# Gathering the expert rows in 512-byte halves and turning them on VectorE in a spectral mixture-of-experts kernel

## The chip, the cores and the metric

One Trainium2 chip, one core. The metric is the device time of one execution in microseconds. Below, TensorE is also called PE, VectorE DVE, ScalarE ACT, GpSimd POOL and SyncE SP, as the profile's rows do.

## What is computed

Two stages follow each other, all in float32:

```python
X = rfft(x, axis=1)                       # x: 8 x 1856 x 256
Yr = Xr @ w_r - Xi @ w_i + b_r            # and Yi, then a soft threshold of 0.01
y = irfft(Yr + 1j * Yi, n=1856, axis=1)   # 14848 rows of 256
g = argmax(y @ w_group); e = argmax(y @ w_expert[g])
h = relu(y @ w1[g, e])                    # 256 -> 1024
out = weight(g, e) * (h @ w2[g, e])       # 1024 -> 256, 16 experts, one per row
```

Each of the 14848 rows goes to one of 16 experts; its output row is the expert's, scaled by two softmax values.

## The kernel before

The first part (to about 440 us of the profile) does the transforms, the routing and the sorting. It writes the transformed rows to a DRAM tensor `ys_d` (one row of 256 values, 1024 bytes, per position) and, for each expert, a list of row numbers and weights to `lst`; the first 512 rows of experts 0 to 3 are worked on there too, in an order written out by hand.

The main part, from about 441 to 1050 us, is the one that the change touches. It works through 40 jobs, numbered 0 to 39 here: expert 3 (256 and 304 rows), expert 1 (432), expert 2 (400), then the largest of the other twelve experts ("rank 0": 384, 384, 336), expert 0 (256, 256), and ranks 1 to 11 with the sizes of `CUTS` (lines 38 to 40). A job's rows lie in tiles of up to 128. For job i the program of the loop at line 1410 says, in this order:

1. `fetch` (lines 535 to 549) gathers the rows of job i+1: for each tile one indirect DMA on GpSimd's queue, one row of 1024 bytes per partition, into tiles `xg` (three buffers of two tiles).
2. The first two tiles of job i-1 go through the second layer (`down_g`, lines 632 to 659: 16 matmuls per tile, then a scaling on ScalarE (L656) and one on VectorE (L657), then an indirect store, L625). The PSUM pool for this has two banks. Jobs of 288, 304, 320, 400 and 416 rows may be "turned": their second layer runs with weights stationary (`turned_g`, L673, one half in front of the first layer of the next job, one behind it) and its result is transposed back (`back_g`, L686) during a later job.
3. The first layer of job i (`up_g`, L578): eight groups of six matmuls; ScalarE takes the high part of the hidden values (L583), VectorE the low part (L585). In some jobs (`split_at`, two jobs ahead of an expert's first) the weights of a later expert are split in eight pieces between these, a cast on ScalarE (L524) and a subtraction on VectorE (L525); where the job has fewer than 384 rows, four of the eight come in the next job.
4. In the jobs that split weights, `dma_next` starts the loads of the expert after, and its row list (`rank_ids`, line 1324, with five small GpSimd operations in `indices`, lines 352 to 359).
5. The leftover tile of job i-1, if it has three, or the second half of a turned job.
6. `prep` (lines 551 to 567) turns the rows of job i+1, so that the 256 features lie on partitions: two TensorE transposes per tile (L561) into PSUM bank `pg`, then ScalarE copies the high part `xth` (L565) and VectorE subtracts to get the low part `xtl` (L566).

TensorE, ScalarE, VectorE and SyncE follow this program order. GpSimd's order is chosen by the compiler within the dependencies. `xq`, which holds `xth` and `xtl`, has two buffers of each. The output tiles `yo` have four. After the loop a flexible loop (line 1463) takes what did not fit in the jobs; it uses `fetch` and `prep` as well.

The core of `up_g`, whose operand order matters here (`w1h`, `w1l` are the high and low weights, stationary):

```python
for ch in range(2):
    for a_, b_ in ((w1h, xth), (w1h, xtl), (w1l, xth)):
        nc.tensor.matmul(o[:, :n], lhsT=a_[:, ch, fs], rhs=b_[:, ch, 0:n], ...)
```

Of the kernel before, what the change touches and what calls it, by code (L numbers as in the profile page):

```python
# [9 lines left out]
F32 = mybir.dt.float32  # L10
F32R = mybir.dt.float32r
# [122 lines left out]


@with_exitstack
def spectral_moe(ctx: ExitStack, tc: tile.TileContext, x, wri, bri, wgate, w1, w2, cst, out):
    nc = tc.nc

    dram = ctx.enter_context(tc.tile_pool(name="dram", bufs=1, space=bass.MemoryType.DRAM))  # L140
# [211 lines left out]
    def indices(ids, pool, both=True):  # L352
        if both:
            nc.gpsimd.tensor_copy(out=ids.gi, in_=ids.ent[:, :, 0])
        tmp = pool.tile([128, 12], F32, name="ixt", bufs=1)[:, 0:ids.n]
        nc.gpsimd.tensor_scalar(out=tmp, in0=ids.ent[:, :, 0], scalar1=0.0, scalar2=float(NPAD + 1), op0=ALU.is_equal, op1=ALU.mult)
        nc.gpsimd.tensor_scalar_add(out=tmp, in0=tmp, scalar1=-1.0)
        nc.gpsimd.tensor_tensor(out=tmp, in0=tmp, in1=ids.ent[:, :, 0], op=ALU.add)
        nc.gpsimd.tensor_copy(out=ids.si, in_=tmp)

    class Ids:
        def __init__(self, ent, gi, si):
            self.ent, self.gi, self.si, self.n, self.last = ent, gi, si, gi.shape[1], 128

        def cut(self, a_, b_):
            part = Ids(self.ent[:, a_:b_], self.gi[:, a_:b_], self.si[:, a_:b_])
            if b_ == self.n:
                part.last = self.last
            return part
# [134 lines left out]
        nc.sync.dma_start(out=lst[NE * CAP:ROWS], in_=zero[:, 0, :])  # L504
        nc.sync.dma_start(out=ys_d[0:1, :], in_=zero[0:1].rearrange("p c k -> p (c k)"))

    def raw_w(e):
        rows = slice(e * 128, e * 128 + 128) if isinstance(e, int) else bass.ds(e * 128, 128)
        raws = []
        for src in (w1, w2):  # L510
            raw = xp.tile([128, 2048], F32, name="xt")
            nc.sync.dma_start(out=raw, in_=src[rows])
            raws.append(raw)
        return raws
# [20 lines left out]
    def fetch(mp, ids, bufs, rows=NPAD + 1, late=False):  # L535
        n = ids.n
        out_ = []
        for c0 in range(0, n, 2):
            w = min(2, n - c0)
            xg = mp.tile([128, 2, D], F32, name="xg", bufs=bufs)  # L540
            for c in range(w):
                m = ids.rows(c0 + c)
                ins = nc.gpsimd.indirect_dma_start(  # L543
                    out=xg[0:m, c, :], out_offset=None, in_=ys_d[0:rows, :],
                    in_offset=bass.IndirectOffsetOnAxis(ap=ids.gi[0:m, c0 + c:c0 + c + 1], axis=0))
                if late:
                    behind(ins, "stores of the early jobs go first")
            out_.append((xg, w, ids.rows(c0 + w - 1)))
        return out_

    def prep(mp, xgs, n, bufs=None):
        xth = mp.tile([128, 2, n], F32R, name="xth", bufs=bufs)
# [768 lines left out]
    def ranked(k):  # L1321
        return nc.values_load(order_r[:, k:k + 1], engines=sp, min_val=0, max_val=NE - 1)

    def rank_ids(k, ek):
        rows = CUTS[k]
        n = sum((m + 127) // 128 for m in rows)
        ids = Ids(ft.tile([128, n, 2], F32, name=f"ent_r{k}"), ft.tile([128, n], I32, name=f"gi_r{k}"),
                  ft.tile([128, n], I32, name=f"si_r{k}"))
        if any(m % 128 for m in rows):
            nc.gpsimd.memset(ids.ent, 0.0)  # L1330
        parts = part_lists(ids, lambda r, n: bass.ds(ek * CAP + r, n), rows)
        indices(ids, ft)
        return parts

    def half_prep(xgs):
        (xg, _, _), = xgs
# [48 lines left out]
    def dma_next():  # L1385
        if not loads:
            return
        j = loads.pop(0)
        kind, q = jobs[j]
        if kind == "l":  # L1390
            raws[j] = raw_w(q[0])
        else:
            k = q[0]
            ek = ranked(k)
            raws[j] = raw_w(ek)
            rids[k] = rank_ids(k, ek)

    table = flex_table()
# [4 lines left out]
    def turned(i):  # L1403
        return 0 < i < len(jobs) - 1 and jids[i].rows() in TURNED and not turned(i - 1)

    prev, behind_, todo = None, iter(()), []
    x2 = prep(xq, first[0], jids[0].rows())
    for e in (3, 1, 2, 0):
        indices(fids[e][0], ft, False)
    for i, (kind, q) in enumerate(jobs):  # L1410
        ids = jids[i]
        if kind == "r":
            wt = wts["r", q[0]] = jw[i] if i in jw else wts["r", q[0]]
        else:
            wt = wts[q[0]] = jw[i] if i in jw else wts[q[0]]
        if i + 1 < len(jobs) and jobs[i + 1][0] == "r":
            k, part = jobs[i + 1][1]
            jids[i + 1] = rids[k][part]
        nxt = fetch(xp2, jids[i + 1], 3, late=i == 0) if i + 1 < len(jobs) else None
        rest, back = iter(()), behind_  # L1420
        behind_ = iter(())
        if prev is not None:
# [22 lines left out]
            emit(todo, len(todo))  # L1445
        if i == 0 or i in split_at:
            dma_next()
        drain(rest)
        prev = (hs, ids, wt)
        if nxt is not None:  # L1450
# [29 lines left out]
def _layout(x, w_r, w_i, b_r, b_i, w_group, w_expert, w1, w2):  # L1480
# [9 lines left out]
        wg[:, i, :, i, G:G + NE] = w_expert.reshape(G, 8, 32, EG).transpose(1, 2, 0, 3).reshape(8, 32, NE)  # L1490
    wg = np.tile(wg.reshape(8, 64, 64).transpose(1, 0, 2), (2, 1, 1))
    w1s = w1.reshape(NE, 2, 128, F).transpose(0, 2, 1, 3).reshape(NE * 128, 2 * F)
    w2s = w2.reshape(NE, 8, 128, D).transpose(0, 2, 1, 3).reshape(NE * 128, 8 * D)
    named = (("x", xs), ("wri", wri), ("bri", bri), ("wgate", wg.reshape(128, 512)), ("w1", w1s), ("w2", w2s))
    return [(n, np.ascontiguousarray(a)) for n, a in named]


# [19 lines left out]
```

## Time and profile before

| | |
|---|---|
| median of 3 runs | 1058.54 us (1057.88 to 1060.74) |
| the profiled execution | 1058.72 us, span 1056.9 us |
| TensorE | busy 1029.3 us (97%), clock 0.998 of full |
| VectorE | 674.9 us (64%) |
| ScalarE | 491.4 us (46%) |
| GpSimd | 427.3 us (40%) |

The span runs from the first to the last instruction of the core. A busy time is the sum over the times in which an instruction of that engine runs; matmuls are pipelined, so that one lasts longer than the step from its start to the next one's. [...] The chain of waits is followed back from the last instruction, at each step to what released it or to the instruction before it on its engine; what is not on it can change without moving the end until it gets there.

### The profile page before, as it was taken

Reading aid. Unit: us, or ns where it says so; the run is one execution under the profiler, and the core shown is the slowest. Engines: PE = TensorE matmul, PEld = TensorE weight load, DVE = VectorE, ACT = ScalarE, POOL = GpSimd, SP = SyncE. Lnnn points to the kernel's source line nnn. Section 1 sums busy time; section 2 is a strip of 40 time slices with the busy share of each in tenths; the row PEclk is TensorE's granted clock in tenths of the full one; section 3 lists DMA queues with packets and bytes.
Section 4 is the critical chain, followed back from the end, with each engine's and each line's share of the span. In section 5 each row is a group of like instructions: output and inputs, shape, how many; then the busy total and the mean of one; then the engine's idle time right before and its main releaser. Section 6 shows DMA issues by size and latency. Waiting matters only on the chain.

```text
span 1056.9 us, 24666 instructions
## 1 busy us (share of the span) xinstructions
PE 1029.3 (97%) x9688; PEld 901.7 (85%) x9688; DVE 674.9 (64%) x1610; ACT 491.4 (46%) x1273; POOL 427.3 (40%) x600
## 2 busy tenths in 40 slices
PE   8999999999999998999999999999999999999997
PEld 4886777776867887899999999999999999999996
DVE  6778999999898675455365555454645546545632
ACT  2564554554635343344354445444544435445532
POOL 0120162555374668553343433343433443342422
PEclk9999999999999999999999999999999999999999
DMA  9401512421414430233132231331313313233110
GB/s 383 153 3 52 210 62 82 156 88 59 146 60 152 142 110 22 64 133 101 56 136 83 87 121 51 119 118 47 131 42 126 118 58 115 77 103 107 46 37 29
DMA packets 33287, 105.27 MB, mean 100 GB/s; under 512 B 13644, under 2 KB 14393, under 8 KB 26642
## 3 DMA queue, kind: packets, MB, share of 16 engines
q1 hardware_dynamic: 16338, 55.92, 15.3%
q0 software_dynamic: 11936, 30.75, 9.0%
q10 hardware_dynamic: 4896, 17.01, 4.2%
q8 instruction: 77, 1.26, 0.5%
q14 instruction: 40, 0.33, 0.1%
HBM read 71.34 MB, written 32.46 MB: 98 GB/s over the span
## 4 chain that ended last, share of the span: by engine, by line
PE 78%; DVE 11%; issue 3%; POOL 3%; DMA 2%; ACT 1%; ACTq 0%; SPq 0%; POOLq 0%; DVEq 0%
PE ph L578 26%; PE py L651 13%; PE py L652 7%; PE py L673 6%; PE pw L843 5%; PE ph L1003 2%; PE pw L825 2%; PE pg L561 2%; PE bank L761 2%; PE bank L867 2%; PE bank L885 2%; PE bank L435 2%; DVE big L439 1%; PE bank L917 1%; PE bank L1026 1%
## 5 line engine op out<-in xcount | busy, mean ns | idle before, releaser
L578 PE MATMUL ph<-xth,big 128*128 128x256 f32 (+8 forms) x1280 | 290.5, 311 | 0.7 <-ACT xth L565 0.7
L585 DVE SCALAR_TENSOR_TENSOR hl<-ph,hh 128x256 fp32r<-128x256 f32 (+8 forms) x528 | 170.3, 357 | 101.3 <-ACT hh L583 99.6
L578 PEld LDWEIGHTS ph<-xth,big 128*128 128x128 f32 x1280 | 216.6, 188 | 2.7 <-ACT xth L565 0.9
L651 PE MATMUL py<-big,hh 128*128 128x512 f32 (+2 forms) x608 | 218.6, 399 | 0.0
L578 PE MATMUL ph<-xtl,big 128*128 128x256 f32 (+8 forms) x640 | 198.0, 309 | 0.4 <-DVE xtl L566 0.4
L583 ACT ACTIVATE hh<-ph 128x256 fp32r<-128x256 f32 (+8 forms) x528 | 154.0, 333 | 89.9 <-PE ph L578 87.8
L543 POOL DMA_INDIRECT xg<-ys_d,gi_r x92 | 90.7, 986 | 247.0 <-PE pg L561 229.6
L652 PE MATMUL py<-big,hl 128*128 128x256 f32 (+2 forms) x608 | 171.0, 281 | 0.0
L651 PEld LDWEIGHTS py<-big,hh 128*128 128x128 f32 (+2 forms) x608 | 113.0, 186 | 27.0 <-DVE yo L692 0.3
L625 POOL DMA_INDIRECT out_dram<-yo,si_r x92 | 91.5, 995 | 89.3 <-DVE yo L657 44.8
L578 PEld LDWEIGHTS ph<-xtl,big 128*128 128x128 f32 x640 | 120.4, 188 | 0.7 <-DVE xtl L566 0.6
L657 DVE SCALAR_TENSOR_TENSOR yo<-py,ent_r,yo 128x256 f32<-128x256 f32 (+1 forms) x66 | 31.9, 484 | 138.1 <-ACT yo L656 138.1
L652 PEld LDWEIGHTS py<-big,hl 128*128 128x128 f32 (+2 forms) x608 | 113.3, 186 | 0.0
L656 ACT ACTIVATE yo<-py,ent_r 128x256 f32<-128x256 f32 (+1 forms) x66 | 31.3, 475 | 152.9 <-PE py L652 117.5
L673 PE MATMUL py<-hh,big 128*128 128x320 f32 (+4 forms) x320 | 75.3, 315 | 0.0
L809 POOL TENSOR_TENSOR xdl<-xd,xdh 128x512 fp32r<-128x512 f32 (+1 forms) x23 | 28.0, 1217 | 109.0 <-ACT xdh L802 88.4
L525 DVE TENSOR_TENSOR big<-xt,big 128x512 fp32r<-128x512 f32 x104 | 71.3, 686 | 0.5
L843 PE MATMUL pw<-wh,xh 128*128 128x256 f32 x240 | 66.7, 300 | 2.6 <-DVE pw L833 2.6
L524 ACT CAST big<-xt 128x512 fp32r<-128x512 f32 x104 | 64.4, 619 | 0.0
L848 ACT ACTIVATE big<-pw,nlam 128x512 f32<-128x512 f32 x60 | 41.4, 690 | 47.1 <-PE pw L843 46.6
L843 PE MATMUL pw<-wl,xh 128*128 128x256 f32 x240 | 62.1, 281 | 0.0
L843 PEld LDWEIGHTS pw<-wh,xh 128*128 128x128 f32 x240 | 45.1, 188 | 16.3 <-DVE pw L833 6.9
(259 smaller groups left out, 2013.6 us busy)
## 6 DMA issues: line engine op xcount, KB each, us to landing
xt<-in_w_dram SPq DMA_DIRECT2D x34, 1024.0 KB
ys_d<-ysb ACTq DMA_DIRECT2D x32, 512.0 KB
big<-in_x_dram SPq DMA_DIRECT2D x8, 1024.0 KB
xt<-in_x_dram SPq DMA_DIRECT2D x8, 1024.0 KB
xg<-ys_d,gi_r POOLq DMA_INDIRECT x92, 2.8
out_dram<-yo,si_r POOLq DMA_INDIRECT x92, 2.4
CI<-in_cst_dram SPq DMA_DIRECT2D x1, 1088.0 KB
T<-in_cst_dram SPq DMA_DIRECT2D x1, 960.0 KB
```

The source lines that it names most:

```text
L524: nc.scalar.copy(out=wt[:, 2 * i, cs], in_=raws[i][:, cs])
L525: nc.vector.tensor_tensor(out=wt[:, 2 * i + 1, cs], in0=raws[i][:, cs], in1=wt[:, 2 * i, cs].bitcast(F32), op=ALU.subtract)
L543: ins = nc.gpsimd.indirect_dma_start(out=xg[0:m, c, :], out_offset=None, in_=ys_d[0:rows, :], in_offset=bass.IndirectOffsetOnAxis(ap=ids.g ...
L578: nc.tensor.matmul(o[:, :n], lhsT=a_[:, ch, fs], rhs=b_[:, ch, 0:n], start=k == 0, stop=k == 5)
L583: nc.scalar.activation(out=hh[:, f, cs], in_=o[:, cs], func=AF.Relu)
L585: nc.vector.scalar_tensor_tensor(out=hl[:, f, cs], in0=o[:, cs], scalar=0.0, in1=hh[:, f, cs].bitcast(F32), op0=ALU.max, op1=ALU.subtract)
L625: ins = nc.gpsimd.indirect_dma_start(out=out, out_offset=bass.IndirectOffsetOnAxis(ap=ids.si[0:ids.rows(t), t:t + 1], axis=0), in_=ysb, in ...
L651: nc.tensor.matmul(o, lhsT=hh[:, f, ts], rhs=w2b[:, :, f, :], start=f == 0, stop=f == 7, skip_group_check=True)
L652: nc.tensor.matmul(o[:, 0:D], lhsT=hl[:, f, ts], rhs=w2h[:, f, :], start=False, stop=f == 7, skip_group_check=True)
L673: nc.tensor.matmul(o, lhsT=w_[:, f, ds_], rhs=h_[:, f, 0:n], start=f == 0 and h_ is hh and w_ is w2h, stop=f == 7 and h_ is hh and w_ is n ...
L843: ins = nc.tensor.matmul(y, lhsT=a_[:, h, k % 2, j], rhs=t[:, j, h], start=False, stop=a_ is xl and h == 1, skip_group_check=True)
L848: nc.scalar.activation(out=z_of(pr)[:, k], in_=psum["m", pr, k], func=AF.Relu, bias=nlam)
```

## The change

From job 4 on (`DEALT`), the rows are gathered two jobs ahead, by `deal`. Each tile takes two indirect DMAs, each for 64 rows: the row's first 512 bytes go to one partition and its second 512 bytes to another, so that blocks of 32 partitions hold halves of 32 rows. The index lists for this are made by `half_ids`, eight small GpSimd operations per list. Four VectorE transposes (in blocks of 32 x 32) over all tiles of the job then put features on partitions, from SBUF to SBUF (`turn_rows`). The features come to lie in another order than before, so the first layer's weights are read from a copy in that order, `w1q`, prepared outside. `turn_rows` stands ahead of step 5 in the list above, where `prep` stood behind it. Jobs 0 to 3 and the flexible loop keep `fetch` and `prep`.

```diff
-    def raw_w(e):
+    def raw_w(e, first=w1):
...
-        for src in (w1, w2):
+        for src in (first, w2):
...
+    half_rows = ys_d.rearrange("r (h d) -> (r h) d", h=2)
+
+    def half_ids(ids, nm):
+        ids.half = ft.tile([128, ids.n, 2], I32, name=f"half_{nm}")
+        for a_ in range(2):
+            for b_ in range(2):
+                for h in range(2):
+                    q, p = 64 * a_ + 32 * h, 64 * b_ + 32 * a_
+                    nc.gpsimd.tensor_scalar(out=ids.half[q:q + 32, :, b_], in0=ids.ent[p:p + 32, :, 0], scalar1=2.0, scalar2=float(h),
+                                            op0=ALU.mult, op1=ALU.add)
+
+    def deal(ids):
+        xm = xq.tile([128, 4, 2, 128], F32, name="xm")
+        for c in range(ids.n):
+            for b_ in range(2):
+                left = ids.rows(c) - 64 * b_
+                if left > 0:
+                    m = 64 if left <= 32 else 128
+                    nc.gpsimd.indirect_dma_start(
+                        out=xm[0:m, c, b_, :], out_offset=None, in_=half_rows,
+                        in_offset=bass.IndirectOffsetOnAxis(ap=ids.half[0:m, c, b_:b_ + 1], axis=0))
+        return xm.rearrange("p c b d -> p (c b) d")
+
+    def turn_rows(xm, ids):
+        n = ids.rows()
+        xt = xq.tile([128, 2, 8, 64], F32, name="xtf", bufs=1)
+        for a_ in range(2):
+            k = (n - 32 * a_ + 63) // 64
+            for to in range(2):
+                nc.vector.transpose(out=xt[64 * to:64 * to + 64, :, 0:k, 32 * a_:32 * a_ + 32].rearrange("f b c t -> f c b t"),
+                                    in_=xm[64 * a_:64 * a_ + 64, 0:k, 64 * to:64 * to + 64].rearrange("t c (b f) -> t c b f", b=2))
+        xth = xq.tile([128, 2, n], F32R, name="xth")
+        xtl = xq.tile([128, 2, n], F32R, name="xtl")
+        xt = xt.rearrange("p b c t -> p b (c t)")
+        for ts in [slice(i, min(n, i + 256)) for i in range(0, n, 256)]:
+            nc.scalar.copy(out=xth[:, :, ts], in_=xt[:, :, ts])
+            nc.vector.tensor_tensor(out=xtl[:, :, ts], in0=xt[:, :, ts], in1=xth[:, :, ts].bitcast(F32), op=ALU.subtract)
+        return xth, xtl
...
-            raws[j] = raw_w(ek)
+            raws[j] = raw_w(ek, w1q)
...
+    DEALT = jobs.index(("r", (0, 0)))
...
-        nxt = fetch(xp2, jids[i + 1], 3, late=i == 0) if i + 1 < len(jobs) else None
+        nxt = fetch(xp2, jids[i + 1], 3, late=i == 0) if i + 1 < DEALT else None
+        if DEALT <= i + 2 < len(jobs):
...
+            ahead[i + 2] = deal(jids[i + 2])
...
             dma_next()
+        if nxt is None and i + 1 < len(jobs):
+            x2 = turn_rows(ahead.pop(i + 1), jids[i + 1])
         drain(rest)
...
+    w1q = w1.reshape(NE, 2, 2, 2, 32, F).transpose(0, 2, 1, 4, 3, 5).reshape(NE * 128, 2 * F)
```

The remaining lines of the diff make `half_ids` for expert 0's list ahead of the loop and for each rank's in `rank_ids`, and hand each job its columns of them.

## Rows read from the trace of the kernel before

**Rows 1.** Busy time per stretch (x instructions), then clock, DMA share, GB/s.

```profile
core 0: us, PE busy (x) PEld busy (x) DVE busy (x) ACT busy (x) POOL busy (x), PEclk, DMA share, GB/s
500.00:1026.00 526.00, 526.00 (x3426) 497.19 (x3424) 273.67 (x721) 245.53 (x704) 198.59 (x243) 1.00 0.27 90
```

**Rows 2.** Chain of waits from 500 to 1026 us, shares by line.

```profile
by line: PE ph L578 46.3%; PE py L651 24.6%; PE py L652 12.5%; PE py L673 11.4%; PE pg L561 4.0%; PE py L686 1.1%; PE pg L1261 0.1%
```

**Rows 3.** PE's groups, 500 to 1026 us: count, busy, mean ns, idle before.

```profile
L561 PE MATMUL pg<-K,xg 128*128 128x128 f32 (+3 forms) x192 | 26.9, 269 | 0.0
```

**Rows 4.** Chain from 902 to 940 us (jobs 31, 32): start, length, what.

```profile
912.74 7.04 PE ph L578 x48
919.77 0.44 PE pg L561 x4
920.21 3.54 PE py L673 x24
923.75 5.65 PE ph L578 x48
```

**Rows 5.** DVE's transposes by form, whole span: count, busy, mean ns, idle before.

```profile
L439 DVE STREAM_TRANSPOSE big<-bank 128x512 f32<-128x512 f32 x64 | 42.7, 694 | 0.6 <-PE bank L435 0.6
L874 DVE STREAM_TRANSPOSE big<-bank 128x1024 f32<-128x1024 f32 x32 | 38.6, 1230 | 2.9 <-PE bank L867 2.8
```

**Rows 6.** ACT's and DVE's groups that split rows and scale results, by form.

```profile
L524 ACT CAST big<-xt 128x512 fp32r<-128x512 f32 x104 | 64.4, 619 | 0.0
L565 ACT CAST xth<-pg 128x512 fp32r<-128x512 f32 x40 | 23.6, 590 | 31.8 <-PE pg L561 31.3
L565 ACT CAST xth<-pg 128x128 fp32r<-128x128 f32 x4 | 1.1, 272 | 0.0
L566 DVE TENSOR_TENSOR xtl<-pg,xth 128x512 fp32r<-128x512 f32 x40 | 27.6, 689 | 7.1 <-ACT xth L565 5.9
L566 DVE TENSOR_TENSOR xtl<-pg,xth 128x128 fp32r<-128x128 f32 x4 | 1.1, 280 | 0.0
L657 DVE SCALAR_TENSOR_TENSOR yo<-py,ent_r,yo 128x256 f32<-128x256 f32 x64 | 31.0, 484 | 134.1 <-ACT yo L656 134.1
```

**Rows 7.** DVE's timeline around the end of job 31: start, length, what.

```profile
920.85 0.69 DVE L525 TENSOR_TENSOR big<-xt,big 128x512 fp32r<-128x512 f32 x1
921.46 0.69 DVE L566 TENSOR_TENSOR xtl<-pg,xth 128x512 fp32r<-128x512 f32 x1
```

**Rows 8.** Chain from 606 to 622 us (job 10's end).

```profile
610.36 0.23 PE py L651
...
613.18 0.70 PE pg L561 x6
613.88 0.43 PE py L651
...
619.72 2.34 PE ph L578 x16
```

**Rows 9.** DVE's timeline around the end of job 10.

```profile
612.15 0.69 DVE L525 TENSOR_TENSOR big<-xt,big 128x512 fp32r<-128x512 f32 x1
613.73 0.48 DVE L657 SCALAR_TENSOR_TENSOR yo<-py,ent_r,yo 128x256 f32<-128x256 f32 x1 [0.88 <-ACT yo L656]
```

**Rows 10.** DVE's timeline at the end of job 16, and the chain behind it.

```profile
709.35 0.92 DVE L566 TENSOR_TENSOR xtl<-pg,xth 128x512 fp32r<-128x512 f32 x2
...
707.13 0.58 PE pg L561 x6
713.37 7.41 PE ph L578 x48
```

**Rows 11.** POOL's timeline from 866 us: gathers and a store in one queue.

```profile
867.92 0.97 POOL L543 DMA_INDIRECT xg<-ys_d,gi_r  x1 [0.30 <-issue]
869.19 0.95 POOL L543 DMA_INDIRECT xg<-ys_d,gi_r  x1 [0.30 <-PE py L652]
871.70 1.02 POOL L625 DMA_INDIRECT out_dram<-yo,si_r  x1 [0.30 <-issue]
```

**Rows 12.** POOL's groups, 500 to 1026 us.

```profile
L543 POOL DMA_INDIRECT xg<-ys_d,gi_r x87 | 85.9, 988 | 234.6 <-PE pg L561 218.4 <-issue 13.1 <-PE py L651 1.5
L625 POOL DMA_INDIRECT out_dram<-yo,si_r x86 | 85.7, 996 | 69.3 <-DVE yo L657 44.8 <-issue 12.3 <-ACT yo L694 4.9
L356 POOL TENSOR_SCALAR ixt<-ent_r 128x7 f32<-128x7 f32 (+3 forms) x11 | 3.4, 305 | 0.0
```

## What I expect of the change, before it ran

> **What bounds the kernel now.** I read three views in this order: busy time by stretch, the chain of waits, then the groups of instructions. The stretch from 500 to 1026 us is the part that the change touches; TensorE is busy for all 526.00 us of it at the full granted clock (1.00, 2.4 GHz), VectorE for 273.67, ScalarE for 245.53, GpSimd for 198.59 [rows 1]. The chain of that stretch holds TensorE lines alone: 46.3% first layer (L578), 48.5% second layer (L651, L652, L673), and 4.0% L561, the transposes that turn gathered rows [rows 2]. So whatever leaves TensorE here leaves the end, as long as nothing makes TensorE wait; and a wait there is new, because now there is none.
>
> **What leaves TensorE.** Jobs 4 to 39 hold 96 tiles, each with two transposes: the 192 of L561 in the stretch [rows 3]. Their busy time (26.9 us) overlaps their neighbours; on the chain four of them take 0.44 us [rows 4], 0.110 each, and 192 x 0.110 = **21.1 us** (4.0% of 526 is 21.0). With them go 192 weight loads that ran beside the matmuls. Jobs 0 to 3 keep theirs. The first layer's new weight order changes neither the count nor the width of its matmuls: zero.
>
> **What VectorE gets.** Four transposes per job, of 64 partitions x 64k elements, k being 6 for 384 rows, 5 for 320, 4 for 256. No row shows a transpose out of SBUF or one over 64 partitions. The nearest are PSUM to SBUF on 128 partitions: 512 elements 694 ns, 1024 elements 1230 ns [rows 5]. That is 1.047 ns an element and 158 ns fixed, so 384 elements take 0.56 us, 320 0.49, 256 0.43, and the four of a job 2.24, 1.97 or 1.70 us; some 70 us over 36 jobs on an engine that is half idle. Two bounds: below, half of it (two elements at a time); above, twice (the blocks of 64 partitions serialised). I take the rows' line, since the source alone seems to matter little: the subtraction of L566 out of PSUM takes 689 ns for 512 elements and the one of L525 from two SBUF operands 690 [rows 6, 7].
>
> I count full durations one behind the other. An ordinary pair overlaps: L525 lasts 0.69 us and what follows starts 0.60 later [rows 7]. With that overlap in the four transposes too a job's turn is some 0.3 us shorter, and the ten waits below shrink by about 3 us in all. [...]
>
> **What that makes late.** The turn of job i+1 stands on VectorE behind all of job i's hidden subtractions and weight pieces, and ahead of the scaling of the last tiles of job i-1, which stood ahead of the subtraction before. The serial path is: VectorE free, four transposes, 0.1 us hand-over, ScalarE copy of 512 elements 0.62 (L524, from SBUF; L565 from PSUM 0.59), subtraction 0.69, then the shorter second pieces [rows 6]. I went through the 36 jobs with the chain and VectorE's timeline; 26 have room. Ten have not, in three kinds.
>
> Kind one, a 256- or 416-row job follows a turned job that has no leftover tile in front (jobs 31, 34, 36). Job 31 leaves the first layer at 919.77; without the 0.44 us only 3.54 us of L673 lie before job 32, which could start at 923.31 [rows 4]. VectorE ends its last weight piece at 920.85 + 0.69 = 921.54 [rows 7]; plus 1.70 (transposes) = 923.24, plus 0.1 and 0.62 = 923.96, plus 0.05 and 0.69 = 924.70. The second matmul, which reads the low part, wants it at 923.43: 1.3 us. Job 34 repeats it; job 36, with 384 rows next, gives 1.45 by the same sum. Together 4.05.
>
> Kind two, a 384-row job splits weights and the job before it left a third tile (jobs 5, 10, 13). In job 10 the leftover tile runs 610.36 to 613.18, then the first tile of job 10 to 615.99 [rows 8]; the second needs the bank that the leftover's scaling frees, and there are two banks. That scaling now stands behind the turn: VectorE free at 612.15 + 0.69 = 612.84 [rows 9], plus 1.97, 0.72, 0.74, 0.28 and 0.48 = 617.0. Wait 1.0; job 5 (336 rows next) 1.2, job 13 (288) 0.65. Together 2.85.
>
> Kind three, weights are split and there are only two tiles to hide behind (jobs 8, 16, 19, 28). Job 16: VectorE free at 709.35 [rows 10], the low part ready 3.75 us later at 713.1; job 17 starts at 713.37 less the 0.58 us of six transposes, and reads it 0.16 later: 0.2 to 0.4. The four give 0.95.
>
> Sum of new waits 7.85 us. **Net 21.1 - 7.9 = 13.2 us.**
>
> **What GpSimd gets.** The gathers of jobs 4 to 39 become 184 in place of 96 (eight half-tiles are empty: last tiles of 64 or 32 rows). Half as many bytes save nothing there: a gather takes 0.97 us for issuing and the next starts 0.30 later [rows 11]. So 184 gathers and 96 stores x 1.3 = 364 us. The list of each rank gets eight small operations on 32 partitions; nearest is L356, 305 ns [rows 12]; with the five there are now some 4 us per list, 43 for 11, and one list of eight ahead of the loop (2.5 us, with the gathers of job 2 having about that much to spare). 407 of 513 us, 79%. I cost it at nothing: a job's gathers are now issued two jobs ahead, wait only for the turn of the job two before, and have one whole job more to land; stores queued behind them lose at most some 7 us, against four output buffers, 11 us of a job and more. SyncE loads the same bytes by the same descriptors from another tensor: zero. The DMA engines move the same bytes in twice as many row packets; the stretch shows 0.27 of their time used [rows 1]: zero while this lead holds.
>
> ScalarE's copy changes source: 0.03 us, within the sums above. The flexible loop, whose path is unchanged, and the tail behind 1026 us stay.
>
> The profiled execution took 1058.7 us (span 1056.9); 1058.7 - 13.2 = **1045.5 us**. The median of the runs, 1058.54, is 0.2 below that execution, so the forecast is as good against either. About 0.3%, 3.2 us, is what a measurement can tell from none.
>
> **Rivals.**
> - *The turn hides altogether*, because the transposes are cheaper or overlap. For it: the two halves' chains are independent and VectorE is half idle. Against: in ten jobs the arithmetic above has no room. Half the price takes 0.85 to 1.1 us off each of the ten waits: about 1040; all of it hidden: 1037.6. Chance 0.15.
> - *VectorE's turn becomes the bound*, on the other side. If a transposition of 64 partitions costs twice the line, a turn takes 4.5 us in place of 2.2; the ten waits grow by 2 us each, and ten to twelve jobs that now have 0.2 to 1.5 us of room (7, 9, 18, 22, 25, 27, 30, 33, 38 and their like) begin to wait, some 18 us: 7.9 + 20 + 18 = 46 against 21, some 1083. It decides from about 0.75 us per transposition of 384 elements (0.2 us more, ten waits by 0.8 and a few new ones): there the gain is gone. For it: no row shows this form. Against: both measured lengths lie on one line. Chance 0.11, and 0.09 more that it takes most of the gain and leaves it within 0.3%.
> - *GpSimd falls behind.* At 1.3 us a DMA it has 100 us to spare; it bounds the part once a DMA with its pause costs 1.7 us. At 1.8: 280 x 1.8 + 43 = 547 against the 526 of now, 1080. For it: every store waits in the same queue. Against: gathers keep to 0.95 to 1.0 us next to busy VectorE [rows 11, 12]. [...] Chance 0.04.
>
> **How the numbers follow.** Forecast with waits of 4 to 14 us: 0.61. With the first rival that is 0.76 faster; same 0.09; slower 0.15. The likeliest case alone runs from 1041 to 1052. The range for 8 in 10 goes down to 1038 (nothing lost) and up to 1056, where the case without a gain begins.
>
> **What would show it.** Right: L561 drops from 218 to 26; TensorE has waits in the stretch, first of all at jobs 32, 35 and 37 for the low part and at the second tile of jobs 5, 10 and 13, a few microseconds together; four VectorE transposes per job of about 0.43 to 0.56 us; gathers landing a job before their turn. Wrong: transposes of 0.75 us or more, a turn that waits for a gather, GpSimd above 95%, or TensorE waits in jobs that I gave room.

## The result, and the profile after

The changed kernel takes **1064.67 us** (median of 12 runs, 1062.14 to 1070.48) beside 1058.27 (12 runs): a ratio of 1.007, 95% interval 1.0049 to 1.0091. It is slower by 0.7% where I forecast 1045.5, 1.2% faster. The profiled execution took 1062.85 us, span 1061.1.

Busy time by stretch, of the changed kernel; the columns are the stretch, its length, busy time and count of PE, PEld, DVE, ACT and POOL, granted clock, DMA share, GB/s:

```profile
455.00:480.00 25.00, 23.20 (x146) 22.27 (x145) 12.82 (x51) 10.03 (x35) 17.77 (x48) 1.00 0.16 43
480.00:492.00 12.00, 2.19 (x13) 1.51 (x12) 1.17 (x2) 0.78 (x2) 7.93 (x10) 0.65 0.19 51
492.00:500.00 8.00, 8.00 (x33) 6.87 (x33) 0.94 (x2) 0.68 (x2) 1.04 (x1) 0.67 0.01 2
500.00:1026.00 526.00, 517.85 (x3290) 486.43 (x3290) 348.65 (x893) 254.24 (x729) 304.11 (x415) 1.00 0.29 93
```

The last row answers to [rows 1]: TensorE lost 8.15 us of the 526 that it was busy for before, and VectorE and GpSimd took 75 and 106 us more, as the change says. The second row is what the prediction does not have: TensorE works 2.19 of 12 us. Its waits from 430 us on say for what (engine, line, waited for: us in total, times, longest; three waits of 1.8 us together, which the kernel before has too, are left out):

```profile
PE pg L603 <- DMA xg<-ys_d,gi_f: 11.9, 4, 9.8
PE py L693 <- DVE yo L699: 2.4, 3, 1.0
PE ph L620 <- ACT xth L589: 2.4, 3, 1.0
PE ph L620 <- DVE xtl L590: 1.7, 6, 0.3
PE py L715 <- DVE yo L699: 1.6, 1, 1.6
```

L603 is the TensorE transposition of a plainly gathered job, `gi_f` a list of the first experts: these are the rows of jobs 2 and 3, whose path the change leaves alone. GpSimd's timeline shows why they are late (start, duration, engine, line, operation):

```profile
472.65 1.01 POOL L572 DMA_INDIRECT xm<-ys_d,half_r  x1 [0.30 <-issue]
...
486.65 0.94 POOL L572 DMA_INDIRECT xm<-ys_d,half_r  x1 [0.30 <-issue]
487.89 0.95 POOL L546 DMA_INDIRECT xg<-ys_d,gi_f  x1 [0.30 <-issue]
489.15 0.86 POOL L546 DMA_INDIRECT xg<-ys_d,gi_f  x1 [0.30 <-issue]
```

The twelve dealt gathers (L572) of jobs 4 and 5 stand ahead of the last two plain ones (L546) of job 3. Each takes about 0.95 and the next starts 0.30 later, as in [rows 11]; the twelve take 15.2 us (472.65 to 487.89). TensorE's timeline goes on from there:

```profile
490.68 1.08 PE L603 MATMUL pg<-K,xg 128*128 128x128 f32 x4 [9.80 <-DMA xg<-ys_d,gi_f]
...
493.15 0.63 PE L693 MATMUL py<-big,hh 128*128 128x512 f32 x1
...
493.79 0.63 PE L693 MATMUL py<-big,hh 128*128 128x512 f32 x1
...
499.23 0.40 PE L693 MATMUL py<-big,hh 128*128 128x512 f32 x1
...
499.59 0.40 PE L693 MATMUL py<-big,hh 128*128 128x512 f32 x1
```

After 9.8 idle microseconds a pair of the second layer's matmuls takes 0.64 us (493.15 to 493.79), later 0.36 (499.23 to 499.59). The granted clock is 0.50 from 483.63 to 497.28, and 1.00 ahead of that and behind it; the 0.67 of the row from 492 to 500 is a mixture of the two. By the pairs' times some 2.45 us are lost in this way, an estimate. The traces give the clock as a share: at 0.50 the 768 columns of a pair pass in 0.64 us, 1.2 a nanosecond; the 2.4 GHz that the prediction has beside 1.00 is twice that rate, an estimate.

The new instructions, grouped by line and shape (count, busy us, mean ns, idle before):

```profile
L583 DVE STREAM_TRANSPOSE xtf<-xm 64x384 f32<-64x384 f32 x58 | 33.0, 570 | 0.6
L583 DVE STREAM_TRANSPOSE xtf<-xm 64x320 f32<-64x320 f32 x26 | 13.1, 503 | 0.3
L583 DVE STREAM_TRANSPOSE xtf<-xm 64x256 f32<-64x256 f32 x58 | 25.4, 438 | 0.6
L572 POOL DMA_INDIRECT xm<-ys_d,half_r x176 | 172.5, 980 | 132.6 <-DVE xtf L583 87.1 <-issue 43.6 <-DMA ent_r<-lst 0.9
```

These are the prices that the prediction took from [rows 5] and [rows 11]. The 176 gathers and 8 more for expert 0 (`half_f`) are the 184 that it counted.

One more reading, worked out from the traces, is how much later than in the trace of before the first layer of a job starts. For job 3, first before and then after:

```profile
486.60 0.34 PE L578 MATMUL ph<-xth,big 128*128 128x400 f32 x1
```

```profile
499.94 0.34 PE L620 MATMUL ph<-xth,big 128*128 128x400 f32 x1
```

| kernel | job 2 | job 3 | job 4 | job 39 | job 3 to 39 |
|---|---|---|---|---|---|
| the changed kernel | +0.40 | +13.34 | +14.51 | +3.09 | -10.25 |
| deals behind job 3's gathers (run 10) | +6.76 | +6.76 | +7.93 | -3.37 | -10.13 |
| and half indices behind them too (run 12) | -3.84 | -3.84 | -1.80 | -13.30 | -9.46 |
| and no turning (run 13) | -0.46 | -0.47 | -1.13 | -23.05 | -22.58 |
| halves alone (run 14) | -1.74 | -1.74 | -1.74 | -1.04 | +0.70 |

So the changed kernel gains 10.25 us in its main part, where 13.2 was forecast, and has lost 15.4 before it gets there (job 0, ahead of all that the change touches, starts at -2.04; over the traces here it lies between -3.9 and +2.8, the kernel before in run 7 at -2.1). The runs below are where the other rows come from.

### The profile page after: what moved, and what is told of

The parts are those of the page before. It is cut to its first block, busy times and chain, and to the rows that moved or that the text cites. A ratio compares the mean times of both kernels' runs of the same rounds, so it can differ in the third digit from the quotient of the medians.

```text
span 1061.1 us, 24712 instructions
## 1 busy us (share of the span) xinstructions
PE 1013.6 (96%) x9496; PEld 883.9 (83%) x9496; DVE 742.5 (70%) x1754; ACT 491.6 (46%) x1273; POOL 539.8 (51%) x792
## 3 DMA queue, kind: packets, MB, share of 16 engines
q1 hardware_dynamic: 16338, 55.92, 15.2%
q8 instruction: 76, 1.25, 0.5%
## 4 chain that ended last, share of the span: by engine, by line
PE 41%; DVE 7%; issue 4%; POOL 2%; ACT 1%; DMA 1%; DVEq 0%; POOLq 0%; ACTq 0%
PE ph L620 20%; PE py L693 11%; PE py L694 5%; PE py L715 5%; DVE big L528 2%; DVE hl L627 2%; DVE xtf L583 2%; POOL xm L572 1%; POOL out_dram L667 1%; ACT xth L589 1%; DVE xtl L590 1%; DMA xm<-ys_d,half_r 0%; ACT hh L625 0%; PE py L728 0%; DMA xg<-ys_d,gi_f 0%
## 5 line engine op out<-in xcount | busy, mean ns | idle before, releaser
L572 POOL DMA_INDIRECT xm<-ys_d,half_r x176 | 172.5, 980 | 132.6 <-DVE xtf L583 87.1
L667 POOL DMA_INDIRECT out_dram<-yo,si_r x92 | 95.2, 1035 | 65.1 <-issue 27.1
L589 ACT CAST xth<-xtf 128x512 fp32r<-128x512 f32 (+5 forms) x59 | 28.4, 518 | 103.6 <-DVE xtf L583 103.6
L583 DVE STREAM_TRANSPOSE xtf<-xm 64x384 f32<-64x384 f32 (+3 forms) x144 | 72.8, 505 | 1.5
```

What stands on the lines that cost most here:

```text
L572: nc.gpsimd.indirect_dma_start(out=xm[0:m, c, b_, :], out_offset=None, in_=half_rows, in_offset=bass.IndirectOffsetOnAxis(ap=ids.half[0:m, ...
L583: nc.vector.transpose(out=xt[64 * to:64 * to + 64, :, 0:k, 32 * a_:32 * a_ + 32].rearrange("f b c t -> f c b t"), in_=xm[64 * a_:64 * a_ + ...
L667: ins = nc.gpsimd.indirect_dma_start(out=out, out_offset=bass.IndirectOffsetOnAxis(ap=ids.si[0:ids.rows(t), t:t + 1], axis=0), in_=ysb, in ...
```

## Experiments

### Runs 1 to 4: the start mended, the halves alone, the turn left out

Run 1 puts the dealt gathers of jobs 4 and 5 behind the last plain one on GpSimd's queue:

```diff
+                    if plain:
+                        tc.add_manual_dep(ins.ins, fetched[-1], queued, reason="plain gathers go first")
...
-            ahead[i + 2] = deal(jids[i + 2])
+            ahead[i + 2] = deal(jids[i + 2], i + 2 < DEALT + 2)
```

> The twelve dealt gathers of jobs 4 and 5 are put behind the last plain gather (job 3) on GpSimd's queue; all else is the changed kernel (1064.7 us). Theory (order on GpSimd's queue): the 9.8 us that TensorE waits for job 3's last rows goes, and with it the stretch at a granted clock of 0.65 to 0.67 behind it, in which the second layer's matmuls cost some 2.45 us more. 1064.7 - 9.8 - 2.45 = about 1052.4, 0.994 of the kernel before; the wait for job 2's rows (some 2 us, behind the half indices) stays. Rival A (the half indices of the first list hold the queue, and the dealt gathers only happened to stand there): job 3's rows stay late, 1062 to 1065. Rival B (GpSimd has too many gathers at whatever place: the wait goes elsewhere): the wait at job 3 goes, and jobs 4 to 7 wait for their own rows instead, by 5 to 12 us: 1058 to 1064.

Run 2 moves the half indices of expert 0's list behind it as well, from ahead of the loop:

```diff
-    half_ids(fids[0][0], "f0")
-    halves(fids[0][1], fids[0][0])
...
+        if i + 2 == jobs.index(("l", (0, 0))):
+            half_ids(fids[0][0], "f0", True)
+            halves(fids[0][1], fids[0][0])
```

> As the first run, and the eight half-index operations of expert 0's list, too, stand behind the last plain gather. Theory (order on GpSimd's queue): the wait of some 2 us for job 2's rows goes as well, so some 2.1 us below the first run, about 1050.3 (0.992 of the kernel before), and the part from job 4 on keeps its gain of 11.4 us. Rival A (half indices hold the queue): nearly all of the loss goes only here, 1050 with the first run still above 1060. Rival B (too many gathers at whatever place): within 1 us of the first run, and both above 1057, with TensorE waits for gathered rows in jobs 4 to 7.

Run 3 is the kernel before with this in `fetch`, from job 4 on:

```diff
+                    for h in range(2):
+                        nc.gpsimd.indirect_dma_start(
+                            out=xg[0:m, c, h * 128:h * 128 + 128], out_offset=None, in_=half_rows,
+                            in_offset=bass.IndirectOffsetOnAxis(ap=ids.half[0:m, c0 + c, h:h + 1], axis=0))
```

> The kernel before with one thing of the change: from job 4 on each gather is two of 512-byte halves, laid down in the old layout, with two index operations per list; the transposes stay on TensorE, and the weights keep their order. Theory (order on GpSimd's queue, no shortage of it): the number of gathers costs nothing where they are not in front of something due; within 3 us of the kernel before, 1055 to 1061, unless its dealt gathers, too, are placed ahead of job 3's rows, which a look at the queue shows, and then up to 12 us more with TensorE's wait at job 3 and nowhere else. Rival B (too many gathers at whatever place): 5 to 15 us slower, 1063 to 1073, with TensorE waits for gathered rows spread over jobs 4 to 39.

Run 4 is run 2 without the turn:

```diff
-                nc.vector.transpose(out=xt[64 * to:64 * to + 64, :, 0:k, 32 * a_:32 * a_ + 32].rearrange("f b c t -> f c b t"),
-                                    in_=xm[64 * a_:64 * a_ + 64, 0:k, 64 * to:64 * to + 64].rearrange("t c (b f) -> t c b f", b=2))
...
+        xt = xm.rearrange("p c d -> p (c d)")[:, 0:2 * n].rearrange("p (b t) -> p b t", b=2)
```

> The second run without the four VectorE transposes: the hidden parts are cut straight from the gathered rows, so the turning of the rows is left out of the computation. It measures what the turn costs the end, which the prediction put at 7.85 us of new waits. Theory: TensorE's waits for VectorE and ScalarE (8.8 us in the changed kernel) go nearly all, so some 8 us below the second run, about 1042, where 21.1 us less than the kernel before would be 1037.2; what lies between stays in the queue's order and in late rows. Rival (the turn is hidden anyway, and the main part gives its gain back elsewhere): within 2 us of the second run.

Measured, all on chip 9, beside 1064.49 for the kernel before: run 1 1145.39 (ratio 1.0747, 95% interval 1.0724 to 1.077), run 2 1146.13 (1.0759, 1.0735 to 1.0783), run 3 1150.10 (1.0799, 1.0776 to 1.0822), run 4 1127.48 (1.0604, 1.058 to 1.0629). No theory had this. TensorE loses time in most jobs of the main part. ScalarE's timeline of run 1, in one job's first layer, and then that of the changed kernel in the same job:

```profile
617.22 0.55 ACT L628 ACTIVATE hh<-ph 128x256 fp32r<-128x256 f32 x2 [0.43 <-PE ph L623]
621.05 1.89 ACT L628 ACTIVATE hh<-ph 128x256 fp32r<-128x256 f32 x8 [3.28 <-PE ph L623]
```

```profile
603.02 0.55 ACT L625 ACTIVATE hh<-ph 128x256 fp32r<-128x256 f32 x2 [0.44 <-PE ph L620]
604.06 0.55 ACT L625 ACTIVATE hh<-ph 128x256 fp32r<-128x256 f32 x2 [0.49 <-PE ph L620]
605.11 0.55 ACT L625 ACTIVATE hh<-ph 128x256 fp32r<-128x256 f32 x2 [0.50 <-PE ph L620]
```

TensorE finished a group every 1.04 us in both. In run 1 ScalarE began none of three finished groups for 3 us, then did four at once, and TensorE stood meanwhile for `ph`, which VectorE (`hl`) had not read: 1.06 us up to 622.40, and from 430 us on 26.8 us in 19 such waits, the longest 4.5. I counted this over the main part: for each of the 320 groups of the first layer (eight in each of 40 jobs), how late ScalarE starts, that is its start less the later of two ends, that of the matmul that releases it and that of the last work that ScalarE had finished by then.

### Runs 5 to 9: whose loss is it?

Runs 5 and 6 are the changed kernel unedited, and run 1's kernel again.

> The changed kernel itself, not edited, as a control beside the next run. The first four runs came out 60 to 85 us above the kernel before (1064.5 beside them), the one with the halves alone (1150.1) too, which leaves the order on GpSimd's queue as it was; their loss lies in every job of the main part, where ScalarE begins pieces up to 3.3 us after the profile shows what they wait for as done. Theory C (that loss belongs to the chip on which those four ran, with 184 gathers in place of 96, and not to the edits): where the next run comes out above 1130, this one does too, 1130 to 1150; where the next run comes out near 1052, this one is 1062 to 1070. Theory D (the edits brought it): this one 1062 to 1070 and the next one about 1145 on the same chip.

> The same kernel as the first run (the twelve dealt gathers of jobs 4 and 5 behind job 3's last plain gather), once more, beside the unedited changed kernel. Theory C (the chip): 10 to 14 us below the run beside it, whatever that is: about 1052 where that is 1064, about 1133 or more where that is 1145. Theory D (the edit): about 1145, 80 us above the run beside it.

1138.74 (1.0713, 1.0655 to 1.0772) and 1136.60 (1.0702, 1.0664 to 1.0739), again on chip 9, beside 1061.63. The unedited kernel is as slow: the loss is the chip's with this kind of kernel, and not the edits' (theory C). Run 6 is only 2 below, not 10 to 14: the rest drowns in it, though TensorE's wait for plain rows is down from 11.2 us in run 5's trace to 1.3.

Run 7 is the kernel before, unedited. Run 8 is the kernel before with a second gather beside each, to a tile that nothing reads. Run 9 is run 2 with VectorE's load eased (weight pieces over two jobs, the turn in the middle of the first layer). The cut of run 8, then that of run 9:

```diff
+                    xs = mp.tile([128, 128], F32, name="xs", bufs=4)
+                    nc.gpsimd.indirect_dma_start(
+                        out=xs[0:m, :], out_offset=None, in_=half_rows,
+                        in_offset=bass.IndirectOffsetOnAxis(ap=ids.gi[0:m, c0 + c:c0 + c + 1], axis=0))
```

```diff
-        every = 1 if todo or ids.rows() < 384 else 0
+        every = 1 if todo or ids.rows() < 384 or i in split_at and i >= DEALT else 0
...
+            if f in (2, 3, 4, 5):
+                next(turn, None)
```

> The kernel before, not edited, with its trace, on the chip on which the changed kernel takes 1138.7. What is looked at is how promptly work that waits for a semaphore begins: in the changed kernel there ScalarE begins pieces of the first layer up to 3 us after the matmul that releases them, and the trace has only 3 or 4 of the 16 landing marks of most gathers. Theory C (gathers, twice as many of them, are what this chip does not take): here all is prompt, 16 landing marks a gather, span about 1060, no TensorE wait between 500 and 1026. Rival E (the chip is always late, and the kernel before merely hides it): late pieces and missing marks here too.

> The kernel before with a second gather beside each gather from job 4 on: 512-byte rows into a scratch tile that nothing reads; the real gather keeps its whole rows of 1024 bytes, there are no half indices, no other layout, no dependence of any work on the second one. Theory C (the number of gathers in the main part, whatever their size and place): as slow as the run with the halves alone, 1120 to 1150. Rival F (the halves themselves, that is rows cut in two that land in one tile, or their index operations): within 5 us of the kernel before, 1056 to 1067.

> The second run's order on GpSimd's queue; in addition the weight pieces of every splitting job from job 4 on are spread four per job over two jobs, and the four transposes of a turn are sent to VectorE in the middle of the first layer instead of behind it. It keeps the 184 gathers. Theory C: on the chip of the first six runs about 1125 to 1140, still 60 us above the kernel before, because only the number of gathers matters there; on a chip that takes them (the one of the first comparison) 1043 to 1047. If VectorE's turn were the cause of the loss, this one falls by 40 us or more below the 1146 of the second run on either.

They ran on chip 8, beside 1060.93: run 7 1059.35 (one run), run 8 1137.98 (1.0707, 1.0645 to 1.0769), run 9 1088.51 (1.0254, 1.0206 to 1.0303). The count over the traces; "beside" means that the releasing matmul ended while GpSimd had an indirect DMA in hand, or within 0.1 us before or 0.5 us after:

| trace | chip | over 0.5 us late, of 320 | of these beside an indirect DMA | longest | beside one, of all 320 |
|---|---|---|---|---|---|
| before, first comparison | not known | 0 | | 0.15 | 118 |
| the changed kernel, first comparison | not known | 1 | 1 | 1.57 | 261 |
| run 7, before | 8 | 15 | 15 | 3.21 | 115 |
| run 5, the changed kernel | 9 | 72 | 71 | 4.62 | 237 |
| run 8, spare gathers | 8 | 40 | 39 | 6.97 | 176 |
| run 3, halves alone | 9 | 74 | 73 | 7.05 | 186 |

Run 7 decides between rival E and theory C: the chip is late under the kernel before too, and most gathers lack some of the marks that the profile keeps of a DMA's landing (8.8 marks an indirect DMA on average, 15.9 in the first comparison's trace of before); theory C expected neither. But its span is 1057.5, and TensorE is busy 525.57 of the 526 us: there its 15 late groups are hidden. In run 7, 115 of the 320 groups end beside an indirect DMA, and all 15 late ones are among them. With twice the gathers the coincidence says less, since most groups end beside one. Run 8 rules out halves, layout and half indices as what it takes: gathers that nothing waits for are enough on such a chip. Run 9 missed theory C's 1125 to 1140. It fell by 58 us below run 2's time (on another chip), which its text called the mark of a cause in VectorE's turn; I read it otherwise, since run 8 has no turn at all, and run 4, without the turn, still lost 63 us: earlier pieces and turns are slack, and slack is what a late hand-over uses up. That the slack is what helped run 9 is argued, and no run separates it. What in the chip holds the hand-over back was not found; and since chips 8, 6, 4 and 0 were each used at one time only, chip and time are not told apart there.

### Runs 10 to 14: chips that hand over promptly

Run 10 is run 1's kernel, run 11 run 9's.

> The kernel of the first and the sixth run once more, because the chip decides: in the traces of chips 8 and 9 work released by a semaphore begins up to 4.6 us late, nearly always next to an indirect DMA of GpSimd (71 of 72 pieces of ScalarE that were more than 0.5 us late in the unedited changed kernel), while in the first comparison's trace one piece of 320 was. On a chip without such lateness the theory of the queue's order says 1052.4 (0.994 of the kernel before, between 0.991 and 0.997), rival B (too many gathers at whatever place) 1058 to 1064. On a chip with it: 1130 to 1150 again, and the trace must show 15 or more pieces over 0.5 us late.

> The kernel of the ninth run once more, beside it. On a chip without late hand-overs 1043 to 1047 (0.985 to 0.989 of the kernel before): the queue's order costs nothing and the waits of kinds two and three go. On a chip with them 1085 to 1095 as before.

On chip 6, beside 1057.41: run 10 **1052.19** (0.994, 0.9921 to 0.996) and run 11 **1040.16** (0.9821, 0.9772 to 0.9869, below the 1043 to 1047 expected); 1 and 0 of 320 groups over 0.5 us late. The queue's theory had 1052.4 for run 10. GpSimd's timeline of run 10: job 3's rows are asked for first.

```profile
476.80 1.02 POOL L546 DMA_INDIRECT xg<-ys_d,gi_f  x1 [0.39 <-PE ph L623]
478.12 0.88 POOL L546 DMA_INDIRECT xg<-ys_d,gi_f  x1 [0.30 <-issue]
479.30 0.97 POOL L573 DMA_INDIRECT xm<-ys_d,half_r  x1 [0.30 <-issue]
```

The order alone is then worth 1.3% (1.007 to 0.994; the intervals lie apart), and rival B falls. Run 11 is the fastest kernel of the study that leaves nothing out, 1.8% below the one before.

Runs 12 to 14 repeat runs 2, 4 and 3.

> The kernel of the second run once more, for a chip without late hand-overs (the tenth run gave 1052.2 on one, the queue's theory said 1052.4). Theory: the remaining wait at job 2 goes too, about 1050 (0.993 of the kernel before, 0.990 to 0.996), and the eleventh run's other 10 us (1040.2) are the weight pieces and the early turn. On a chip with late hand-overs: 1140 to 1150, and 60 or more pieces over 0.5 us late.

> The kernel of the fourth run once more: the second run's order, and the turning of the rows is left out of the computation. On a chip without late hand-overs: the waits for VectorE's turn (7.85 us by the prediction, 8.8 in the changed kernel's trace) go nearly all, 1041 to 1043, 7 to 9 below the run beside it; by the rival (the turn is hidden anyway) within 2 us of it. On a chip with them: 1120 to 1135.

> The kernel of the third run once more: the kernel before with gathers in halves from job 4 on and nothing else of the change. On a chip without late hand-overs the theory of the queue's order says that 184 gathers cost nothing by themselves: 1055 to 1061; rival B 1063 to 1073. On a chip with them: 1135 to 1155, as the third run (1150) and the one with spare gathers (1138), both from such chips.

On chip 4, beside 1057.61: run 12 **1046.82** (0.9884, 0.9834 to 0.9935), run 13 1034.10 (0.9753, 0.9701 to 0.9804) and run 14 **1057.59** (0.9996, 0.9975 to 1.0018); at most 1 group of 320 over 0.5 us late.

Run 14: doubled gathers cost nothing by themselves here, as the prediction said. Busy time by stretch, of run 14 and, under it, of run 13:

```profile
500.00:1026.00 526.00, 525.63 (x3423) 497.02 (x3422) 273.43 (x720) 245.13 (x704) 292.51 (x355) 1.00 0.28 90
```

```profile
500.00:1026.00 526.00, 525.16 (x3367) 497.36 (x3366) 278.92 (x740) 250.28 (x723) 303.49 (x416) 1.00 0.28 91
```

Run 12 moves nothing beyond run 10 but eight small operations and gains more than I gave it: some 1050 was expected (the ratios' intervals just overlap, 0.9921 to 0.996 and 0.9834 to 0.9935). Run 10's trace tells why. There those operations wait on GpSimd's queue, and job 2's rows behind them:

```profile
457.01 1.44 POOL L563 TENSOR_SCALAR half_f<-ent_f 32x4 int32<-32x4 f32 x6 [4.66 <-DMA xg<-ys_d,gi_f]
...
463.51 1.07 POOL L546 DMA_INDIRECT xg<-ys_d,gi_f  x1 [0.17 <-PE ph L623]
```

TensorE waits 2.3 us for these rows (1.84 and 0.44), the clock falls (0.86 granted between 455 and 480 us), and from job 1 to job 2 the delay against the trace of before grows by 5.43 us. In the changed kernel the same wait is 1.8 us (1.36 and 0.44), and the clock stays at 1.00.

Run 13 against run 12 is the price of VectorE's turn: **12.7 us** by time, 13.1 by the jobs' starts in their traces, where the prediction had 7.85 and the run's text 7 to 9. Run 13 also shows what the transposes were worth: 22.58 us from job 3 to job 39, with no wait of TensorE in between; that is 0.118 each, for the 0.110 of [rows 3, 4].

### Runs 15 and 16: the kinds of wait taken apart

TensorE's waits in run 12 (from 430 us on, without those that the kernel before has):

```profile
PE py L720 <- DVE yo L704: 2.4, 1, 2.4
PE py L698 <- DVE yo L704: 2.4, 3, 1.0
PE ph L625 <- ACT xth L594: 2.3, 3, 0.9
PE ph L625 <- DVE xtl L595: 1.8, 6, 0.3
```

Run 15 puts the turn behind the scaling of the leftover tiles (`drain(rest)` ahead of `turn_rows`); run 16 spreads the weight pieces alone (the line `every` of run 9).

> The twelfth run's kernel (1046.8) with one thing moved: VectorE's turn stands behind the scaling of the leftover tiles of the job before, where the subtraction stood in the kernel before, and not ahead of it. The prediction's kind two (the second tile of jobs 5, 10 and 13 waits for the bank that the scaling behind the turn frees; 3.2 us by the jobs' steps in the twelfth run's trace, and 2.4 more at job 4): those waits go, TensorE waits no more for yo except the 0.7 that the kernel before has, and it comes out 4 to 6 us below, 1041 to 1043 (0.983 to 0.987 of the kernel before). Rival: the scaling delays the turn by as much as the tile gained, so that the waits come back for the low part of the rows: within 1.5 us of the twelfth run. On a chip with late hand-overs: above 1085, and nothing of the two is told apart.

> The twelfth run's kernel with the weight pieces of all splitting jobs from job 4 on spread four per job over two jobs, so that VectorE is free some 2 to 3 us earlier when a splitting job's turn begins; the turn stays where the change has it. Kinds two and three (jobs with weight pieces, 3.2 and 2.3 us by the steps) should go nearly all and kind one (4.9 us; jobs without leftover tile, whose last piece is late) stay at best by half: 1040 to 1043. If the place of the turn alone matters and not the pieces ahead of it, within 1.5 us of the twelfth run, and the 6.7 us that the eleventh run gained come from the early turn.

On chip 0, beside 1057.96: run 15 1062.01 (1.0043, 1.0016 to 1.0071) and run 16 1047.60 (0.9913, 0.9887 to 0.994); 1 and 2 of 320 groups over 0.5 us late, so this chip is prompt. Waits of run 15, then of run 16:

```profile
PE ph L625 <- ACT xth L594: 7.0, 8, 3.1
PE ph L625 <- DVE xtl L595: 4.3, 14, 0.3
PE py L720 <- ACT hh L630: 2.3, 1, 2.3
```

```profile
PE py L720 <- DVE yo L704: 2.1, 1, 2.1
PE ph L625 <- ACT xth L594: 2.1, 3, 0.7
PE ph L625 <- DVE xtl L595: 1.0, 3, 0.3
PE py L698 <- DVE yo L704: 0.7, 2, 0.4
```

Run 15 misses by 20 us and goes beyond its rival. The waits for yo did go: jobs 5, 10 and 13 step 0.3 us behind run 13's at most, for 1.23, 1.25 and 0.71 in run 12. But the low parts come late in 14 places, and jobs 36 and 37 alone step 11.6 us behind run 13's. In job 36 ScalarE stood on an output buffer:

```profile
986.27 0.47 ACT L741 ACTIVATE yo<-py,ent_r 64x256 f32<-64x256 f32 x1 [7.21 <-DMA out_dram<-yo,si_r]
```

In the chain of waits the store of that buffer is this one, behind five dealt gathers from 977.20 on in the same queue:

```profile
983.65 1.03 POOL L672 DMA_INDIRECT out_dram<-yo,si_r  x1 [0.30 <-issue]
```

It landed 2.46 us after its start. The prediction had four output buffers cover such a store. With this order they don't.

Run 16 does what it should in the jobs that split weights: summed over the steps of jobs 5 to 38 the loss against run 13 falls from 10.4 to 7.0 us: kind one stays (4.9 to 4.8), kind two halves (3.2 to 1.5), kind three nearly goes (2.3 to 0.8). The time does not show these 3.4 us: 1047.60 is no better than run 12's, and the two intervals overlap. The expected 1040 to 1043 is missed, and by time the run meets its rival (within 1.5 us of run 12). Its profiled execution started job 0 6.8 us later than run 12's, ahead of all in which the two kernels differ, which is twice that. By the traces, from job 3 to job 39, run 12 gains 9.5 us, run 16 13.2 and run 11 17.5, so that the pieces bring some 4 and the early turn some 4; by time run 11 is 0.6 points of ratio ahead of run 12, with intervals that still overlap.

## Why the prediction was wrong

The step that failed is **"What GpSimd gets"**, in one clause of it: "I cost it at nothing". Forecast and measurement are 19.6 us apart (13.2 faster, 6.4 slower); this step cost 15.4, and new waits that were forecast too small (below) another 4.5, of which the transposes gave 1.5 back; the other 1.2 these terms don't explain. I asked whether GpSimd has the time over the whole part, and it has (runs 14 and 10). I did not ask what a plain gather stands behind. GpSimd's order is the compiler's, so twelve gathers whose rows are due at jobs 4 and 5 went ahead of two that job 3 needed next, and eight index operations ahead of job 2's. The lead of "one whole job more" that the prediction counted as cover was bought from the plain gathers at the seam. GpSimd's timeline of before has the first of these two gathers of job 3 at

```profile
464.78 1.08 POOL L543 DMA_INDIRECT xg<-ys_d,gi_f  x1 [0.87 <-issue]
```

and the changed kernel at 487.89, 23.1 us later: 15.2 for the twelve dealt gathers (some 1.27 each, as in [rows 11]) and 8 for the index operations and what comes late with them. TensorE wanted the rows 9.80 before 490.68, so 13 us were covered and 9.8 were not. From job 0 to job 3 the loss is 15.4 us, of which 9.8 and 2.1 are waits and 2.45 the clock. With the order mended, the same kernel takes 1046.8 (run 12), and the forecast of 1045.5 is 1.3 from it. That nearness is in part luck: from job 3 to job 39 run 12's trace gains 9.5 us and not 13.2, and the interval of its ratio is 5 us wide to either side.

The clause "2.5 us, with the gathers of job 2 having about that much to spare" was wrong as well: the eight operations not only ran, six of them stood 4.4 us waiting on the queue (4.66 in run 10, the row above), with job 2's gathers behind them.

**Transposes leave TensorE**: 21.1 forecast, 22.58 found.

**VectorE's turn**: 0.57, 0.50 and 0.44 us for the 0.56, 0.49 and 0.43 taken. To count full durations was the author's choice, and it held: the four do not overlap, those of 384 elements start 0.57 to 0.59 apart, and the overlap of [rows 7] does not carry over. It is not that transposes never overlap: in the trace of before the 128-partition transposes of L439 follow each other after 0.60 us at 0.68 each, and in the changed kernel the first of the four overlaps what stands ahead of it by some 0.08. The other three start 0.013 after the end of the one before. What makes this difference no run shows. For the hand-overs of 0.1 and 0.05 us that the prediction took, ScalarE's copy starts 0.09 after the last transposition's end in 27 of the 36 jobs (0.03 in seven), and VectorE's subtraction 0.03 after the copy.

**New waits**: 7.85 forecast, 12.3 by the steps of the changed kernel against run 13's (22.58 less 10.25), 12.7 by time. Kind one is 4.9 (forecast 4.05), at the ends of jobs 31, 34 and 36 as named and the low parts right behind. Kind two is 3.2 (2.85) at jobs 5, 10 and 13. Kind three is 2.4 (0.95): the four named, and 0.3 at two jobs that I gave room. The turn of job 4, which I passed over, takes the other 1.8, at the end of job 3. The listed waits make only 8.1 of this. The rest lies at the same places, since a listed wait is idle time alone. Job 5's:

```profile
554.29 0.28 PE L694 MATMUL py<-big,hl 128*128 128x256 f32 x1
555.56 0.51 PE L693 MATMUL py<-big,hh 128*128 128x512 f32 x1 [0.99 <-DVE yo L699]
555.90 0.28 PE L694 MATMUL py<-big,hl 128*128 128x256 f32 x1
```

It is listed as 0.99, but from start to start the late matmul comes after 1.27 us in place of 0.12 in run 13, and the next after 0.34 in place of 0.24. Such steps around the late matmuls, which are over 0.06 us longer than run 13's, make 12.4 us in all, and all other steps together none.

**Net of the main part**: 13.2 forecast, 10.25 found. **Rivals**: VectorE is no bound (348.65 us busy of 526); GpSimd did fall behind, yet not as I priced it (by rate), but by order.

## What to carry to other kernels

Where the compiler orders a queue, an earlier issue for one part is a later one for its neighbour: at the seam between an old and a new scheme, list what stands ahead of each old instruction, and pin the order where something is due. The load of 79%, as forecast, said nothing here of the queue's order. And measure a close result on more than one chip: here a kernel that gains 0.6% on one loses 7% on another.

## What was not expected of the hardware

On chips 8 and 9 ScalarE begins groups up to 7 us after the matmul that releases them, nearly always beside an indirect DMA of GpSimd (table above): 15 of 320 groups with the gathers of before, 72 in the changed kernel, and at most 2 in the first comparison and on chips 0, 4 and 6. The kernel before hardly feels it (1059 to 1064 us on both, 1057 to 1058 elsewhere); kernels with twice the gathers lose 28 (run 9) to 86 us (run 3).

TensorE's granted clock fell to 0.50 at 483.63 us of the changed kernel's trace, 2.75 us into an idle time of 9.8, and stayed there to 497.28. In run 10's it was 0.86 in the mean from 455 to 480 us, around idle times of 1.84 and 0.44 that end at 467.28: three matmuls of 304 columns take 0.76 us from 468.33 to 473.65, for 0.42 at 457.53. With idle times of 1.36 and 0.44 at that place the changed kernel kept 1.00.
